# Attention and two expert layers: v's maximum in a scratch of its own, and new places for the loads and tasks of the first heads

## The chip, the core and the metric

The kernel runs on one core of a Trainium2 chip. The metric is the device time of one execution in microseconds (us). PE is the matmul engine and PEld its weight load, DVE the vector engine, ACT the scalar engine, POOL the GpSimd engine, and SP the engine whose queue issues nearly all transfers (DMAs) here. Each engine works through its own instructions in the order in which the program gives them, and waits where an input or a buffer is not ready.

## What is computed

Three parts follow one another: attention with a hashing mask, then two expert layers. Cut to what matters:

```python
q_bits = (einsum('bhsd,dk->bhsk', q, proj) > 0)      # 6 bits per row, the same for k
mask   = q_bucket[:, :, :, None] == k_bucket[:, :, None, :]
scores = where(mask, q @ k.T / sqrt(64), -1e9);  attn = softmax(scores)
x  = (attn @ v)                                       # 2 batches x 8 heads, 768 rows, 64 columns
h  = x @ w_in;   g = P(h) / (Q(h) + 1e-6);   x = g @ w_out      # 1536 x 512 x 2048
h  = x @ w2_in;  g = h - tanh(h);            out = g @ w2_out
```

## The kernel before

**Heads and places.** The attention runs over 16 heads `h` of 768 rows; each head has six blocks `j` of 128 keys. Every step of a head is a task with a number, its place: `T` holds the places of a usual head relative to its first block (six places per head), `EARLY` those of heads 0 to 3, and `MOVE` adds a correction to a single task, by name. `FILL` lists groups of idle matmuls (`fill`, L966, 122 columns each) that only keep PE busy. The tasks are sorted by place and issued in that order (`on`, L1027 and on), and each engine keeps it. So a changed number changes the order in the queues of the engines that the task touches, and nothing else.

**The steps of a head.** `load_qk` (L713) issues the load of k and q of the head (384 KB, two buffers). `split_hi` (L756, ACT) rounds them to a high part `A`, `split_lo` (L760, POOL, for head 0 DVE) makes the rest `Bl`. `place` (L768, L769) sends two parts of `A` into the operands `TBk` and `TBq`, and `out_of place` (L775, four issues) the others into `TA`. `bits` (L785, PE) makes the hash bits; `out_of bits` (L789, L792 for head 0; L795 and the transfer L798 for the others) turns them into mask rows of `TBk` and `TBq`. `smax` (L810, PE) and `out_of max` (L814, DVE) give the maximum of every row; `put_max`, for head 0 `put_half`, turns the six maxima by a PE transpose into the bank `sbank` (L825), DVE reads them out (L831), and SP sends them into a row of `TBq` (L832). Then come `scores` (L930, PE), `out_of e` (L933, ACT exponential), `round_e` (L942 ACT, L944 DVE), `rest_e` (L953, POOL) and `attend` (L985 to L988, PE). A ring of three double PSUM banks serves `bits`, `smax` and `scores`.

**v.** `load_v` (L850) loads v of two heads (384 KB), `vmax` (L854, DVE) takes each partition's maximum, `vall` (L859) sends these into one row, and `out_of vback` (L865 to L869, four small DVE instructions) makes a scale of them. It works in two numbers of `sbank`, on partition 64, in columns that lie inside the stretch which `put_part` uses on partitions 0 to 5:

```python
o = SH + D + 2 * (pr % 2)
x = sbank[64:65, o:o + 2]
```

`out_of vagain` (L873) sends the scale to all partitions; `vhi` (L894, ACT) and `vlo` (L900 or L904, ACT, then L901 on POOL or L905 on DVE) need it, and so does `vmean_of` (L911, PE), which also writes to `sbank`.

**Order on SP at the start:** `load_qk` 0, the projection, `load_v` 0, `place` 0, `load_qk` 1, `out_of place` 0, `place` 1, `vall` 0, `load_qk` 2, `out_of place` 1, the maxima of head 0 in two halves, `vagain` 0, the bits of head 1, `load_qk` 3, `place` 2, `out_of place` 2, the bits of head 2, `load_v` 1, `load_qk` 4, `place` 3.

Of the kernel before, what the change touches and what calls it, by code (L numbers as in the profile page):

```python
# [10 lines left out]
F32, F32R, F16, BF16, I32 = DT.float32, DT.float32r, DT.float16, DT.bfloat16, DT.int32  # L11
# [5 lines left out]
B, H, S, D = 2, 8, 768, 64  # L17
# [5 lines left out]
SH = S // 2  # L23
# [12 lines left out]
EH_ACT_LAST = (768, 0, 768, 384, 768, 768)  # L36
EL_DVE_LAST = (640, 0, 0, 384, 128, 768)

FILL = ((199.95, 71), (91.54, 25), (-29.26, 33), (-6.1, 72), (-0.79, 4), (-23.35, 19), (8.78, 3), (-23.45, 5), (1.45, 8))

VLO_POOL = (0, 1)

# [228 lines left out]
 'vlo 10': 0.153,  # L271
 'smax 1 3': -0.091,
 'scale 1 1': -2.1579,
 'smax 0 2': -1.278,
 'out_of e (13, 2)': -0.263,
 'load_qk 2': 3.2764,
 'vall 0': 12.2053,
 'place 1': -0.1816,
 'round_e 8 5': 0.213,
 'out_of vmean 15': 0.073,  # L280
 'out_of place 1': 0.9139,
# [5 lines left out]
 'fill 19': -1.743,  # L287
 'out_of max (0, 2)': 0.006,
 'out_of max (13, 5)': 0.393,
 'load_qk 1': 0.1764,  # L290
 'attend 8 2': -0.953,
 'load_v 0': -1.2766,
 'attend 4 2': -0.953,
# [18 lines left out]
 'normalize 15': -0.377,  # L312
 'vhi 8': -0.1387,
 'attend 12 1': -0.883,
 'vhi 2': 0.553,
 'vlo 1': 0.073,
 'out_of place 3': -0.2893,
 'scores 13 0': 0.07,
 'round_e 15 5': 0.3926,
 'vmax 0': 10.6854,  # L320
 'scores 9 1': -0.055,
 'out_of max (0, 0)': 1.02,
 'smax 0 0': 1.318,
 'out_of bits 0': 10.916,
 'out_of e (15, 1)': -0.473,
 'scores 15 1': -0.055,
 'round_e 14 4': 0.006,
 'out_of e (14, 4)': -0.01,
 'load_v 1': 2.2916,
 'put_max 15': 0.633,  # L330
 'out_of put 15': 0.625,
 'out_of max (2, 5)': -0.7062,
 'smax 2 5': -0.4082,
 'out_of e (9, 2)': -0.263,
 'attend 13 0': -0.2423,
 'halves 0 1': 0.753,
# [7 lines left out]
 'out_of e (15, 0)': 0.8687,  # L344
 'round_e 15 0': 0.3407,
 'scale 0 1': 1.277,
 'out_of max (15, 4)': -1.2373,
 'smax 15 4': -0.9393,
 'scores 15 0': 0.948,
 'put_max 1': 0.203,  # L350
 'out_of put 1': 0.155,
# [7 lines left out]
 'out_of vmean 0': 0.403,  # L359
 'vhi 12': -0.023,  # L360
 'place 0': -0.568,
 'split_hi 0': -0.27,
 'smax 1 4': -0.153,
 'out_of e (13, 5)': -0.473,
 'scores 13 5': -0.055,
 'rest_e 15 4': 2.093,
 'vmean_of 1': 0.703,
 'out_of vmean 1': 0.553,
 'bits 0': 11.964,
 'smax 0 1': 0.024,  # L370
 'join 1 1': -1.01,
 'round_e 14 5': 1.0,
 'rest_e 14 5': 0.592,
 'attend 0 3': 0.193,
 'attend 14 1': -0.008,
 'scores 15 5': 0.413,
 'scores 7 0': 0.073,
 'round_e 0 2': 0.3044,
 'scale 3 1': -0.383,
 'attend 0 4': -0.103,  # L380
 'halves 2 0': 0.203,
 'scores 1 3': -0.093,
 'halves 2 1': 0.4539,
 'round_e 15 1': -0.003}
J0 = 2
YSQ = (0.9, 4, 3.5)
GC = dict(sub=0.7, hi=1.35, lo=1.95)
# [43 lines left out]
def tile_fn(ctx: ExitStack, tc: tile.TileContext, kq, v, proj, w1i, w1o, a_, b_, w2i, w2o, out):  # L431
# [236 lines left out]
    with ExitStack() as actx:  # L668
        actx.enter_context(tc.manual_schedule(engines={getattr(nc, e).engine for e in ORDERED}))
        ap = actx.enter_context(tc.tile_pool(name="ap", bufs=1))  # L670
# [4 lines left out]
        sbank = sgl.tile([P, 512], F32, name="sbank")  # L675
# [181 lines left out]
        def vall(pr):  # L857
            row = ap.tile([1, 2 * P], F32, name=f"vrow{pr}", tag="vrow", bufs=1)
            nc.sync.dma_start(row.rearrange("o (p h) -> o p h", h=2), vmx.pop(pr))  # L859
            sc = ap.tile([1, 2], F32, name=f"vs1{pr}", tag="vs1", bufs=2)  # L860

            def back():
                o = SH + D + 2 * (pr % 2)
                x = sbank[64:65, o:o + 2]
                nc.vector.tensor_reduce(x, row.rearrange("o (p h) -> o h p", h=2), axis=AX.X, op=ALU.max)  # L865
                xi = x.bitcast(I32)
                nc.vector.tensor_scalar(xi, xi, 0x7F800000, None, op0=ALU.bitwise_and)
                nc.vector.tensor_scalar(x, x, 2.0 ** -87, 2.0 ** -12, op0=ALU.max, op1=ALU.mult)
                nc.vector.reciprocal(sc, x)  # L869

            def again():
                vs = ap.tile([P, 2], F32, name=f"vsc{pr}", tag="vsc", bufs=3)
                nc.sync.dma_start(vs, sc.unsqueeze(1).to_broadcast([1, P, 2]))  # L873
                for j in range(2):
                    vsc[2 * pr + j] = vs[:, j:j + 1]

            outs["vback", pr], outs["vagain", pr] = back, again
# [161 lines left out]
        def on(place, fn, *args):  # L1039
            tasks.append((place + MOVE.get(move_name(fn, args), 0), len(tasks), fn, args))  # L1040
# [48 lines left out]
        for u in range(NE):  # L1089
            for fi in range(FG):  # L1090
                t = end + TT["h0"] + TT["slot"] * (4 * u + fi)
                on(t, h_mm, u, fi)
                for n, f in zip("abcde", (stage_a, stage_b, stage_c, stage_d, stage_e)):
                    on(t + TT[n], f, u, fi)
        for t, n in FILL:
            on(t, fill, n)
# [27 lines left out]
        for _, _, fn, args in sorted(tasks, key=lambda x: x[:2]):  # L1124
            name = fn.__name__
# [555 lines left out]
```

## Time and profile before

| | |
|---|---|
| median of 3 runs | 750.57 us (748.86 to 751.51) |
| profiled execution | 748.52 us, span 746.8 us |
| TensorE clock, mean of the span | 0.993 of full |
| busy: PE, DVE, ACT, POOL | 729.5 us (98%), 616.5 us (83%), 551.8 us (74%), 538.4 us (72%) |
| chain that ended last | PE 74%, DVE 14%, ACT 4%, DMA 3%, POOL 2% |

A timeline row has start and length in us, engine, line, operation and tiles, and in brackets the idle time ahead of it and what ended that. A wait row names who waited for whom, with sum, count and longest. PEclk is the clock granted to PE as a share of full speed. A busy share is an average over stages with different limits, so a stage is read from its own rows.

### The profile page before, as it was taken

Reading aid. Unit: us, or ns where it says so; the run is one execution under the profiler, and the core shown is the slowest. Engines: PE = TensorE matmul, PEld = TensorE weight load, DVE = VectorE, ACT = ScalarE, POOL = GpSimd, SP = SyncE. Lnnn points to the kernel's source line nnn. Section 1 sums busy time; section 2 is a strip of 40 time slices with the busy share of each in tenths; the row PEclk is TensorE's granted clock in tenths of the full one; section 3 lists DMA queues with packets and bytes.
Section 4 is the critical chain, followed back from the end, with each engine's and each line's share of the span. In section 5 each row is a group of like instructions: output and inputs, shape, how many; then the busy total and the mean of one; then the engine's idle time right before and its main releaser. Section 6 shows DMA issues by size and latency. Waiting matters only on the chain.

```text
span 746.8 us, 14449 instructions
## 1 busy us (share of the span) xinstructions
PE 729.5 (98%) x5406; PEld 598.1 (80%) x5406; DVE 616.5 (83%) x1034; ACT 551.8 (74%) x979; POOL 538.4 (72%) x459
## 2 busy tenths in 40 slices
PE   8899999999999999999999999999999999999997
PEld 6788888888888888888888888887887676767664
DVE  7689998999968987899899999989666867778765
ACT  1688889988998787766776677688576768677652
POOL 2679898998998897777787789959646366364531
PEclk8999999999999999999999999999999999999999
DMA  7665546565420321212112212101030220311003
GB/s 197 170 163 141 151 115 173 163 150 166 124 86 30 113 85 57 70 61 69 56 57 86 75 39 70 44 2 56 29 114 32 83 85 29 113 57 57 29 29 140
DMA packets 43373, 66.56 MB, mean 89 GB/s; under 512 B 6164, under 2 KB 29812, under 8 KB 43304
## 3 DMA queue, kind: packets, MB, share of 16 engines
q1 hardware_dynamic: 43160, 65.52, 29.8%
q8 instruction: 42, 0.69, 0.4%
q14 instruction: 27, 0.22, 0.1%
q10 hardware_dynamic: 144, 0.13, 0.1%
HBM read 43.00 MB, written 3.15 MB: 62 GB/s over the span
## 4 chain that ended last, share of the span: by engine, by line
PE 74%; DVE 14%; ACT 4%; DMA 3%; POOL 2%; issue 2%; SPq 0%; POOLq 0%; ACTq 0%; DVEq 0%
PE y L1486 16%; PE h L609 16%; PE y L1179 16%; PE h2b L1391 6%; DVE mx L814 4%; PE st L930 4%; PE h2e L1391 4%; PE h2a L1391 4%; PE sm L810 2%; DVE TBk L795 1%; DVE eh L944 1%; POOL x L1365 1%; ACT e L933 1%; PE bits L785 1%; PE pv L985 1%
## 5 line engine op out<-in xcount | busy, mean ns | idle before, releaser
L953 POOL TENSOR_TENSOR el<-e,eh 128x768 f16<-128x768 f32 (+2 forms) x95 | 151.4, 1613 | 22.5 <-DVE eh L944 10.0
L1486 PE MATMUL y<-wS,g 128*128 128x512 f16 (+1 forms) x438 | 102.8, 378 | 0.0
L933 ACT ACTIVATE e<-st,lnk 128x768 f32<-128x768 f32 x96 | 86.1, 898 | 19.0 <-PE st L930 16.9
L814 DVE TENSOR_REDUCE mx<-sm 128x1 f32<-128x768 f32 x96 | 90.0, 950 | 9.5 <-PE sm L810 8.6
L1470 POOL TENSOR_TENSOR g<-tmp,g 128x384 f16<-128x384 f32 x48 | 44.0, 917 | 67.0 <-ACT g L1465 55.4
L665 POOL TENSOR_TENSOR G<-vec,G 128x512 fp32r<-128x512 f32 x44 | 57.2, 1306 | 26.0 <-ACT G L660 25.9
L1486 PEld LDWEIGHTS <-g 128*128 128x128 f16 x438 | 38.5, 98 | 45.6 <-issue 6.3
L1179 PE MATMUL y<-G,wO 128*128 128x512 f32 x288 | 67.1, 391 | 0.0
L1509 DVE SCALAR_TENSOR_TENSOR ya<-y,few,ya 128x512 f32<-128x512 f32 (+1 forms) x73 | 54.0, 741 | 15.0 <-PE y L1486 14.1
L1179 PE MATMUL y<-G,wE 128*128 128x512 f32 x288 | 66.3, 390 | 0.0
L609 PE MATMUL h<-x,wO 128*128 128x512 f32 x288 | 66.3, 390 | 0.0
L1179 PEld LDWEIGHTS y<-G,wE 128*128 128x128 f32 x288 | 54.1, 188 | 11.2
L609 PEld LDWEIGHTS h<-x,wO 128*128 128x128 f32 x288 | 54.1, 188 | 11.2
L1179 PEld LDWEIGHTS y<-G,wO 128*128 128x128 f32 x288 | 53.9, 188 | 11.3 <-POOL G L665 0.3
L942 ACT CAST eh<-e 128x384 f16<-128x384 f32 (+2 forms) x95 | 60.9, 642 | 1.7
L985 PEld LDWEIGHTS <-eh 128*128 128x128 f16 x576 | 53.1, 97 | 10.0 <-issue 9.9
L1391 PE MATMUL h2b<-x,wE 128*128 128x384 f32 x288 | 60.3, 344 | 0.8 <-ACT x L1359 0.8
L985 PE MATMUL pv<-VB,eh 128*128 128x65 f16 x540 | 57.8, 194 | 0.0
L988 PE MATMUL pv<-VB,el 128*128 128x65 f16 x540 | 57.0, 192 | 0.8 <-POOL el L953 0.8
L986 PE MATMUL pv<-VB,eh 128*128 128x64 f16 x540 | 57.4, 195 | 0.0
L930 PE MATMUL st<-TA 128*128 128x384 f32 x192 | 56.4, 375 | 0.5 <-DVE mx L814 0.3
L810 PE MATMUL sm<-TBk,TBq 76*128 76x384 f32 x192 | 52.2, 357 | 3.2 <-DVE TBq L792 2.1
(202 smaller groups left out, 2039.0 us busy)
## 6 DMA issues: line engine op xcount, KB each, us to landing
raw<-in_w1i_dram SPq DMA_DIRECT2D x16, 512.0 KB
raw<-in_w1o_dram SPq DMA_DIRECT2D x16, 512.0 KB
raw<-in_w2i_dram SPq DMA_DIRECT2D x16, 512.0 KB
raw<-in_w2o_dram SPq DMA_DIRECT2D x16, 512.0 KB
kq<-in_kq_dram SPq DMA_DIRECT2D x16, 384.0 KB
TA<-A SPq DMA_DIRECT2D x32, 192.0 KB
TA<-Bl SPq DMA_DIRECT2D x32, 192.0 KB
vraw<-in_v_dram SPq DMA_DIRECT2D x8, 384.0 KB
```

Source lines behind the costliest of these rows:

```text
L609: nc.tensor.matmul(ps, l[:, dc], r, start=(n == 0), stop=(n == 11))
L810: nc.tensor.matmul(ps[:, n], TBq[h][0:76, j * P:(j + 1) * P], TBk[h][0:76, n * SH:(n + 1) * SH], start=True, stop=True)
L814: d = nc.vector.tensor_reduce(mx[h][:, j:j + 1], ps, axis=AX.XY, op=ALU.max)
L930: nc.tensor.matmul(ps[:, n], l[h][0:k, j * P:(j + 1) * P], q[h][0:k, n * SH:(n + 1) * SH], start=(k == P), stop=(k < P))
L933: outs["e", (h, j)] = lambda: nc.scalar.activation(halved(e), ps, AF.Exp, scale=1.0 / math.sqrt(D), bias=lnk)
L942: nc.scalar.copy(t[:, 0:r], e[:, 0:r])
L953: nc.gpsimd.tensor_sub(l[:, r:NK], e[:, r:NK], eh[h, j][:, r:NK])
L985: nc.tensor.matmul(out(t), a[:, t], vb[:, j, 0:PW], start=False, stop=False, skip_group_check=True)
L986: nc.tensor.matmul(out(t)[:, 0:D], a[:, t], vb[:, j, PW:PW + D], start=False, stop=False, skip_group_check=True)
L1179: nc.tensor.matmul(ps, l[:, o], r, start=(n == 0), stop=(n == 11))
L1391: nc.tensor.matmul(banks[n, k], w_in(j, l)[:, o:o + P], x[:, r, dt], start=new and z == 0, stop=z == 5, skip_group_check=not new)
L1486: nc.tensor.matmul(ps[:, c], g[:, l, o], r[:, c], start=(z == 0), stop=(z == 5))
```

## The change

One line of code moves: the two numbers of `vback` get a small SBUF tile of their own, `vx`, in place of a corner of `sbank`. Everything else is numbers in `FILL` and `MOVE`. Sorted out by queue they do this:

- SP: `load_qk` 1 goes ahead of `place` 0, right behind `load_v` 0. `load_qk` 2 and then `vall` 0 go ahead of `place` 1. `load_v` 1 goes ahead of `out_of place` 2 and the bits of head 2. `place` 3 goes ahead of `load_qk` 4.
- PE: idle matmuls ahead of the first `bits` 71 in place of 57; 3 new ones behind the third `smax` of head 0; the groups of 4 (before the first `scores`), of 8 (behind `scores` 0 1) and of 3 go, and one single matmul comes. `scores` 0 4 goes ahead of `smax` 2 0, `scores` 0 5 ahead of `smax` 2 1 and `vmean_of` 1; `attend` 0 3 ahead of `bits` 3, `smax` 2 5 ahead of `smax` 2 4, `scores` 1 4 ahead of `vmean_of` 2. Later a few swaps in heads 6, 7 and 13 to 15: among them `smax` 15 4 ahead of `attend` 13 0, `attend` 13 4 ahead of `smax` 15 5, `put_max` 15 ahead of two `scores` and `attend` 13 5.
- ACT: `split_hi` 3 goes ahead of the exponential of block 0 1; `vhi` 2 behind the exponential of block 1 1; `vlo` 15 about two blocks earlier; one exponential of block 1 2 and one stage of the first expert layer ahead of a neighbour.
- DVE: the maximum 2 2 ahead of `vback` 1, 2 5 ahead of 2 4, the bits of head 4 ahead of a rounding, 15 4 and `vlo` 15 earlier, `out_of put` 15 earlier.
- POOL: `split_lo` 3 ahead of `rest_e` 0 1.

The diff, cut:

```diff
-FILL = ((199.95, 71), (91.54, 25), (-29.26, 33), (-6.1, 72), (-0.79, 4), (-23.35, 19), (8.78, 3), (-23.45, 5), (1.45, 8))
+FILL = ((199.95, 71), (91.54, 25), (-29.26, 52), (-6.1, 72), (-23.35, 19), (6.47, 1), (-11.01, 3))
...
- 'load_qk 2': 3.2764,
+ 'load_qk 2': -0.8365,
- 'place 1': -0.1816,
+ 'place 1': 12.6501,
- 'load_qk 1': 0.1764,
+ 'load_qk 1': -1.4262,
- 'vhi 2': 0.553,
+ 'vhi 2': 1.023,
- 'vmax 0': 10.6854,
+ 'vmax 0': 11.55,
- 'load_v 1': 2.2916,
- 'put_max 15': 0.633,
- 'out_of put 15': 0.625,
+ 'load_v 1': 2.2339,
+ 'put_max 15': -0.2439,
+ 'out_of put 15': -0.2519,
...
+ 'split_lo 0': -2.4888,
+ 'out_of max (2, 2)': -0.703,
+ 'smax 2 2': -0.405,
+ 'scores 0 4': -0.444,
+ 'vlo 15': -1.807,
+ 'out_of place 2': 4.8369,
+ 'place 3': -0.893,
+ 'split_hi 3': -1.0739,
+ 'split_lo 3': -1.0569,
+ 'scores 0 5': -0.25,
...
             def back():
-                o = SH + D + 2 * (pr % 2)
-                x = sbank[64:65, o:o + 2]
+                x = ap.tile([1, 2], F32, name=f"vx{pr}", tag="vx", bufs=2)
                 nc.vector.tensor_reduce(x, row.rearrange("o (p h) -> o h p", h=2), axis=AX.X, op=ALU.max)
```

## Rows read from the trace of the kernel before

**Rows 1.** Busy by stretch: us, then PE, PEld, DVE, ACT, POOL; PEclk, DMA, GB/s
```profile
0.00:20.00 20.00, 16.47 (x150) 14.25 (x151) 14.14 (x33) 3.78 (x4) 4.55 (x20) 0.83 0.75 196
...
60.00:80.00 20.00, 19.72 (x272) 18.27 (x269) 18.30 (x29) 18.21 (x31) 18.48 (x12) 1.00 0.64 164
```
**Rows 2.** Timeline of SP, the first 30 us: start, length, issue
```profile
0.74 0.39 SPq L713 DMA_DIRECT2D kq<-in_kq_dram  x1
...
1.65 0.43 SPq L850 DMA_DIRECT2D vraw<-in_v_dram  x1
...
5.76 0.59 SPq L713 DMA_DIRECT2D kq<-in_kq_dram  x1
...
12.14 0.46 SPq L768 DMA_DIRECT2D TBk<-A  x1
...
13.35 0.54 SPq L859 DMA_DIRECT2D vrow<-vm  x1
...
17.08 1.64 SPq L832 DMA_DIRECT2D TBq<-mr  x2
...
18.81 0.55 SPq L873 DMA_DIRECT2D vsc<-vs  x1
...
20.31 0.51 SPq L713 DMA_DIRECT2D kq<-in_kq_dram  x1
...
27.55 0.50 SPq L850 DMA_DIRECT2D vraw<-in_v_dram  x1
```
**Rows 3.** Timeline of ACT, 0 to 30 us
```profile
3.66 0.83 ACT L756 CAST A<-kq 128x768 fp32r<-128x768 f32 x1 [1.65 <-DMA kq<-in_kq_dram]
...
11.29 0.83 ACT L756 CAST A<-kq 128x768 fp32r<-128x768 f32 x1 [6.80 <-DMA kq<-in_kq_dram]
...
21.50 0.62 ACT L894 ACTIVATE VB<-vraw,vsc 128x384 f16<-128x384 f32 x1 [2.12 <-DMA vsc<-vs]
...
23.03 0.88 ACT L933 ACTIVATE e<-st,lnk 128x768 f32<-128x768 f32 x1
...
25.32 0.90 ACT L933 ACTIVATE e<-st,lnk 128x768 f32<-128x768 f32 x1 [0.87 <-PE st L930]
...
28.63 0.82 ACT L756 CAST A<-kq 128x768 fp32r<-128x768 f32 x1
```
**Rows 4.** Timeline of DVE
```profile
6.97 1.07 DVE L789 TENSOR_SCALAR TBk<-bits,thr,amp 13x768 fp32r<-13x768 f32 x1
...
16.98 0.16 DVE L869 RECIPROCAL vs<-sbank 1x2 f32<-1x2 f32 x1
...
33.60 0.95 DVE L854 TENSOR_REDUCE vm<-vraw 128x2 f32<-128x768 f32 x1 [2.10 <-DMA vraw<-in_v_dram]
...
41.96 0.96 DVE L814 TENSOR_REDUCE mx<-sm 128x1 f32<-128x768 f32 x1 [1.27 <-PE sm L810]
...
208.33 0.95 DVE L814 TENSOR_REDUCE mx<-sm 128x1 f32<-128x768 f32 x1
```
**Rows 5.** Timeline of PE
```profile
1.08 4.53 PE L966 MATMUL pvw<-ones 128*128 128x122 f16 x57 [1.08 <-DVE q1c L598]
...
8.80 1.32 PE L810 MATMUL sm<-TBk,TBq 76*128 76x384 f32 x6 [2.06 <-DVE TBq L792]
...
15.42 5.23 PE L966 MATMUL pvw<-ones 128*128 128x122 f16 x76
...
210.54 0.27 PE L825 MATMUL sbank<-ident,mx 128*6 128x128 f32 x1
```
**Rows 6.** Waits of PE in 0:60, 100:140 and 140:180: us, times, longest
```profile
PE sbank L911 <- DVE mr L831: 2.3, 1, 2.3
PE sbank L825 <- DVE vs L869: 0.5, 1, 0.5
...
PE sbank L825 <- DVE vs L869: 0.6, 1, 0.6
...
PE sbank L825 <- DVE vs L869: 0.8, 1, 0.8
```
**Rows 7.** PE's clock around its long wait, columns as in the first group
```profile
35.00:36.00 1.00, 1.00 (x14) 1.00 (x12) 1.00 (x2) 0.22 (x1) 0.00 (x0) 0.50 0.08 1
...
38.00:39.00 1.00, 1.00 (x7) 1.00 (x7) 0.77 (x3) 1.00 (x3) 0.00 (x0) 0.99 0.97 285
```

More of the change, by code (lines that the diff above doesn't have):

```diff
@@ L273 @@
  'scale 1 1': -2.1579,
- 'smax 0 2': -1.278,
+ 'smax 0 2': -1.243,
  'out_of e (13, 2)': -0.263,
- 'load_qk 2': 3.2764,
+ 'load_qk 2': -0.8365,
  'vall 0': 12.2053,
- 'place 1': -0.1816,
+ 'place 1': 12.6501,
  'round_e 8 5': 0.213,
@@ L319 @@
  'round_e 15 5': 0.3926,
- 'vmax 0': 10.6854,
+ 'vmax 0': 11.55,
  'scores 9 1': -0.055,
- 'out_of max (0, 0)': 1.02,
- 'smax 0 0': 1.318,
- 'out_of bits 0': 10.916,
+ 'out_of max (0, 0)': 1.061,
+ 'smax 0 0': 1.355,
+ 'out_of bits 0': 10.953,
  'out_of e (15, 1)': -0.473,
@@ L328 @@
  'out_of e (14, 4)': -0.01,
- 'load_v 1': 2.2916,
- 'put_max 15': 0.633,
- 'out_of put 15': 0.625,
- 'out_of max (2, 5)': -0.7062,
- 'smax 2 5': -0.4082,
+ 'load_v 1': 2.2339,
+ 'put_max 15': -0.2439,
+ 'out_of put 15': -0.2519,
+ 'out_of max (2, 5)': -1.1504,
+ 'smax 2 5': -0.8524,
  'out_of e (9, 2)': -0.263,
@@ L346 @@
  'scale 0 1': 1.277,
- 'out_of max (15, 4)': -1.2373,
- 'smax 15 4': -0.9393,
+ 'out_of max (15, 4)': -1.423,
+ 'smax 15 4': -1.125,
  'scores 15 0': 0.948,
@@ L361 @@
  'place 0': -0.568,
- 'split_hi 0': -0.27,
+ 'split_hi 0': -1.3028,
  'smax 1 4': -0.153,
@@ L368 @@
  'out_of vmean 1': 0.553,
- 'bits 0': 11.964,
- 'smax 0 1': 0.024,
+ 'bits 0': 12.001,
+ 'smax 0 1': 0.059,
  'join 1 1': -1.01,
@@ L373 @@
  'rest_e 14 5': 0.592,
- 'attend 0 3': 0.193,
+ 'attend 0 3': 0.187,
  'attend 14 1': -0.008,
@@ L378 @@
  'round_e 0 2': 0.3044,
- 'scale 3 1': -0.383,
+ 'scale 3 1': -0.377,
  'attend 0 4': -0.103,
  'halves 2 0': 0.203,
- 'scores 1 3': -0.093,
+ 'scores 1 3': -0.087,
  'halves 2 1': 0.4539,
- 'round_e 15 1': -0.003}
+ 'round_e 15 1': -0.003,
+ 'smax 8 4': 0.883,
+ 'vmean_of 2': 0.433,
+ 'split_lo 0': -2.4888,
+ 'out_of max (2, 2)': -0.703,
+ 'smax 2 2': -0.405,
+ 'round_e 1 4': 0.143,
+ 'scores 6 4': -0.433,
+ 'scores 0 4': -0.444,
+ 'put_max 2': 0.006,
+ 'out_of max (8, 4)': 0.585,
+ 'attend 6 1': -0.883,
+ 'vlo 15': -1.807,
+ 'out_of place 2': 4.8369,
+ 'round_e 1 1': 0.473,
+ 'rest_e 1 1': 0.065,
+ 'place 3': -0.893,
+ 'split_hi 3': -1.0739,
+ 'split_lo 3': -1.0569,
+ 'smax 15 5': 0.923,
+ 'out_of max (15, 5)': 0.625,
+ 'attend 7 1': -0.953,
+ 'scores 0 5': -0.25,
+ 'rest_e 14 2': 1.212,
+ 'rest_e 14 3': 0.215,
+ 'round_e 7 0': 0.008}
 J0 = 2
```

## The prediction

> **What bounds the kernel now.** I read the busy shares by stretch first. From 60 us on PE works nearly without a gap (19.72 of 20 us), with DVE, ACT and POOL close behind (18.2 to 18.5 of 20); the first 20 us have PE at 16.5 and ACT at 3.8 [rows 1]. So the start is where an engine can win time by order alone, and later an engine that gains must be followed by the others. Next I read the waits of PE. One is long: 2.3 us of `vmean_of` for DVE's read of the maxima. Three times, 0.5, 0.6 and 0.8 us, the transpose of the maxima waits for the last instruction of `vback`, which works in the same bank [rows 6]. Then I asked in the timelines why. DVE reached `vmax` of the second pair of heads 2.10 us before its data: DVE stood still until 33.60 for v, and behind it in DVE's queue stood the read of the maxima that PE waited for [rows 4]. That v had been issued at 27.55 and took 6.0 us to land [rows 2, 4]. [...] The start is a chain of loads. The second head's k and q are issued at 5.76, and ACT has them at 11.29; only then can SP issue `place` 1 at 12.14, and everything queued on SP behind it starts there: v's maximum (13.35), the maxima of head 0 (17.08), v's scale (18.81) [rows 2, 3]. ACT waits 2.12 us for that scale, until 21.50, and its first exponential is at 23.03 [rows 3].
>
> **The second head's load.** It is issued right behind v's, at 1.65 + 0.43 = 2.1 us in place of 5.76 [rows 2]. Its landing isn't in this trace. The first load is used at 3.66 [rows 3]; v and this one follow, 384 KB each, and at the 196 GB/s of the first 20 us [rows 1] each takes 2.0 us: an estimate of 7.7 us. The bounds are 5.0 (2.9 us from issue to use as the first load, 0.74 to 3.66 [rows 2, 3]) and 8.1 (6.0 us as the later v). I take 7.7: three loads then stand in one queue. ACT converts by 8.5, where it did by 12.1 [rows 3], so `place` 1 no longer holds SP. What stands between, the third head's load, v's maximum and the six transfers of `place` 1, is issued at some 0.6 us each [rows 2], all before the maxima are ready. The scale is then issued when DVE has it: 16.98 + 0.16 = 17.14 in place of 18.81, a gain of 1.67 [rows 2, 4]. It landed 2.69 us after its issue (18.81 to 21.50), and the first exponential came 1.53 later [rows 2, 3]; by this it goes from 23.03 to 21.4.
>
> Against it stand 14 more idle matmuls ahead of the first hash bits, 71 in place of 57. At 4.53/57 = 79 ns [rows 5] they are 1.1 us of PE. They end after the bits' inputs are there, and DVE reads the bits at 6.97, behind `vmax` [rows 4], so part of it is covered. I take 0.3 (0 to 1.1): the cover, DVE's work ahead, is about as long as the rest. The exponential also needs the first `scores`: PE's 76 idle matmuls run from 15.42 to 20.65, 69 ns each [rows 5]; without four of them, and 0.3 late, `scores` start at 20.7, about a microsecond ahead of 21.7. Both paths meet there. **Term A: 1.2 us** of 1.3, ends 0 and 1.6.
>
> The group of 8 idle matmuls that goes (8 x 69 ns = 0.55) stands where PE waits for buffers and DVE sets the pace, and the three new ones stand where PE waits for DVE's maxima: nothing either way, and 0.2 to 0.5 if that cover is gone.
>
> **v of the second pair.** `load_v` 1 stood behind the four transfers of `place` 2 and the bits of head 2, at 27.55. It now stands behind `place` 2's first two. The third load before these was issued at 20.31 [rows 2]; about 1.2 us earlier, and with two issues of 0.6 between, v goes out at about 21. With the 6.0 us of before it lands at 27. DVE comes to it at 33.60 - 2.10 = 31.5 [rows 4], by term A at 30.3: 3 us to spare. So DVE's wait goes. Late next is the read of the maxima itself, 0.95 us of `vmax` later; `scores` 0 5, put ahead of `vmean_of`, fills that time on PE. What PE's wait in the rows shows as 2.3 [rows 6] is thus worth DVE's 2.1. **Term B: 2.1**, ends 1.5 and 2.3.
>
> **The clock behind it.** [...] Some 3 us ran at half [rows 7], 1.5 us of PE. DVE was busy through that stretch and only then waited 1.27 us for PE, at 41.96 [rows 4]; the gain can't pass that. **Term C: 0.7**, ends 0 and 1.3.
>
> **The scratch of `vback`.** On SBUF, the transposes of the maxima need not wait for DVE's last step on it: 0.5 + 0.6 + 0.8 = 1.9 us of waits on PE [rows 6]. The four small instructions stay (the last takes 0.16 us [rows 4]). PE wins what it waited; the time at the end gains only where PE was last. DVE with 18.3 of 20 us [rows 1] has little room to follow. **Term D: 0.8**, ends 0 and 1.9.
>
> **Places further on.** Most swaps are of neighbours on PE with the same inputs: nothing, and some tenths where a buffer comes free later. `vhi` 2 goes behind an exponential on ACT, and v's second scale comes 0.96 us later on DVE, as a maximum goes ahead of it; the one covers the other. `put_max` 15 goes ahead of two `scores` and an `attend`. Its last maximum ended at 208.33 + 0.95 = 209.28, the transpose ran at 210.54 [rows 4, 5]: 1.26 us of slack, and the steps that it passes are some 2.5 us of PE. So PE may wait up to 1.3 us there, with `scores` queued behind. **Term E: -0.4**, ends 0 and -1.3.
>
> **Sum:** 1.2 + 2.1 + 0.7 + 0.8 - 0.4 = 4.4 us. From the profiled execution's 748.5 that gives 744.1. That execution lies 2.1 us under the median of the runs; I carry the difference to the median: 750.6 - 4.4 = 746.2.
>
> **Rivals.** *First, the load takes the bandwidth of what is needed sooner.* The second head's 384 KB go ahead of `place` 0, whose transfers the first `smax` needs; it ran at 8.80, released by DVE's mask rows [rows 5], so the transfers were there by then. At 196 GB/s that is 2.0 us [rows 1]; DVE's maxima, the scale and the first exponential would then all be later by up to that, and term A is gone: 4.4 - 1.2 = 3.2, 747.4 us. For it: the two stand in one queue. Against: the load issued at 5.76 took 5.5 us with 768 KB of `TA` issued behind it [rows 2, 3], more than a load alone, so what is issued later shares the engines and doesn't simply queue. [...]
>
> *Second, the other engines keep the pace.* If DVE sets the time from 40 us on, what PE alone gains (C and D) becomes idle time of PE in front of DVE's releases, and `put_max` 15 costs its whole 1.3: 1.2 + 2.1 - 1.3 = 2.0, 748.6 us. For it: DVE at 18.3 of 20 us [rows 1]. Against: DVE waited for PE too, 1.27 us at 41.96 [rows 4].
>
> *Third, slower: a load that is late takes the place of v's.* `split_hi` 3 now stands ahead of the exponential of block 0 1 on ACT, and waits for the fourth load. Before, that load was issued at 20.31 and its conversion ran at 28.63 without a wait [rows 2, 3], so it landed anywhere before that. In my schedule ACT comes to it at 22.8 and is through at 23.7, with the exponential at 24.1 in place of 25.32 [rows 3]. Every microsecond of landing after 22.8 is one more for the exponential, and with it for the buffers of `smax` and `scores` on PE. From a landing at 27.2 the whole gain is gone; at the bound of 28.6 it costs 5.8, and with PE standing still that long 1.5 more for the clock (as in C): 750.6 - 4.4 + 7.3 = 753.5 us. Against it: loads took 2.9 to 6.0 us from issue to use, and issued near 19.5 this one should land by 22.4 to 25.5.
>
> **How the numbers follow.** The forecast has 0.53, the first rival 0.17, the second 0.20, the third 0.10. About 0.3%, 2.25 us, is what a measurement of this kernel tells from no change: faster means under 748.3, slower over 752.8. The forecast counts as faster nearly throughout, the first rival mostly, the second in a third of its cases: 0.51 + 0.13 + 0.06 = 0.70. Slower is nearly the third alone: 0.09. The rest, 0.21, is no change. With all terms at their better ends the gain is 1.6 + 2.3 + 1.3 + 1.9 = 7.1, 743.5, and a microsecond for the scatter of the runs gives 742.5; that all are at their ends at once is unlikely, so no more is added. Above, the second rival with 748.6 and its scatter, and the smaller cases of the third, reach 751.0.
>
> **What would show it.** Right: SP issues the second head's load near 2 us and v's scale near 17.2; ACT's first exponential lies at 21.4 to 22; DVE's wait for v near 31 us is gone and the clock stays at full there; no transpose of the maxima waits for `vback`; DVE's maximum that was at 41.96 comes about 4 us earlier, and the first expert layer begins about 4 us earlier. Wrong: the first `smax`, at 8.80 before [rows 5], later than 9.5 us, ACT waiting for the fourth load ahead of block 0 1's exponential, or PE waiting longer for DVE or ACT between 60 and 200 us than before, with the gain at 42 us larger than that at the end.

## The result, and the profile after

The changed kernel takes 758.35 us (median of 6 runs, 755.60 to 762.55) against 749.19 us (748.51 to 751.51) for the kernel before on the same chip. The ratio is 1.012, interval 1.0098 to 1.0143: slower by some 9 us, where 746.2 with 742.5 to 751.0 was forecast. The profiled execution, the slowest of the six (762.55 us), has a span of 760.7 us, against 746.8; so its rows show somewhat more loss than the median has.

First the page after: busy time by engine, and the chain of work that ended last, by engine. The lines have moved by 24 or 25 places (L825 is L850 now, L609 is L633 or L634).

```profile
PE 736.6 (97%) x5409; PEld 601.3 (79%) x5409; DVE 630.6 (83%) x1034; ACT 551.8 (73%) x979; POOL 539.1 (71%) x459
...
PE 66%; DVE 20%; ACT 5%; POOL 4%; issue 2%; DMA 2%; ACTq 0%; DVEq 0%; POOLq 0%
```

DVE executes the same 1034 instructions as before and is busy 630.6 us in place of 616.5. These 14.1 us are new, and DVE's share of the chain has gone from 14% to 20%. Which instructions grew? Groups of DVE instructions by line and shape, the mask and the scaling before and then all four after: name, shape and count, then busy us in all and mean ns of one.

```profile
L867 DVE TENSOR_SCALAR sbank<-sbank 1x2 int32<-1x2 int32 x8 | 1.4, 172 | 0.3
L868 DVE TENSOR_SCALAR sbank<-sbank 1x2 f32<-1x2 f32 x8 | 1.4, 172 | 0.3
...
L892 DVE TENSOR_SCALAR vx<-vx 1x2 f32<-1x2 f32 x8 | 11.9, 1484 | 0.3
L891 DVE TENSOR_SCALAR vx<-vx 1x2 int32<-1x2 int32 x8 | 5.4, 671 | 0.3
L889 DVE TENSOR_REDUCE vx<-vrow 1x2 f32<-1x256 f32 x8 | 3.2, 401 | 0.1
L893 DVE RECIPROCAL vs<-vx 1x2 f32<-1x2 f32 x8 | 1.2, 153 | 0.3
```

The last four are the small instructions of `vback`. The reduction and the reciprocal take what they took (0.16 us for the reciprocal in [rows 4]). The mask (L891) and the scaling (L892), two numbers each, were 172 ns each in every one of their eight places before; now they are 671 and 1484 ns on average, 17.3 us in place of 2.8. These 14.5 us cover the whole growth of DVE. The timeline says what they wait for. Two stretches of DVE and POOL, after: start and length in us.

```profile
17.95 0.41 DVE L889 TENSOR_REDUCE vx<-vrow 1x2 f32<-1x256 f32 x1
17.97 1.80 POOL L785 TENSOR_TENSOR Bl<-kq,A 128x768 fp32r<-128x768 f32 x1 [6.03 <-ACT A L781]
18.39 1.40 DVE L891 TENSOR_SCALAR vx<-vx 1x2 int32<-1x2 int32 x1
19.83 0.16 DVE L892 TENSOR_SCALAR vx<-vx 1x2 f32<-1x2 f32 x1
...
38.59 0.16 DVE L891 TENSOR_SCALAR vx<-vx 1x2 int32<-1x2 int32 x1
38.73 1.65 POOL L977 TENSOR_TENSOR el<-e,eh 128x768 f16<-128x768 f32 x1 [1.10 <-ACT eh L966]
38.78 1.61 DVE L892 TENSOR_SCALAR vx<-vx 1x2 f32<-1x2 f32 x1
```

At 18.39 the mask begins while POOL is inside an instruction that ends at 19.77; the mask ends at 19.79. Then POOL stands still, and the scaling takes 0.16. At 38.59 it is the other way round: POOL is idle during the mask (0.16), starts at 38.73, and the scaling that begins 0.05 us later ends with POOL, at 40.39. The reduction at 17.95 isn't held, though POOL works through most of it. So on SBUF these two instructions stand still for as long as POOL's current instruction runs. Ten of the sixteen are hit, for 1.40 to 1.76 us each, and each of the ten ends within 0.03 us of a POOL instruction's end. The other six take 0.16: two fall into idle time of POOL, four into the tenth of a microsecond in which one POOL instruction gives way to the next.

PE's waits show who pays. Stretch 60 to 260 us, one row before and two after: us in all, times, longest.

```profile
PE sbank L911 <- DVE mr L831: 0.7, 1, 0.7
...
PE sbank L935 <- DVE mr L856: 5.0, 4, 2.4
PE sbank L850 <- DVE mx L839: 2.6, 1, 2.6
```

The old waits of the transpose for `vback` [rows 6] are gone, as intended. In their place PE waits longer for what is queued behind `vback` on DVE: the maxima and their read-out. One such chain, DVE and PE, after:

```profile
58.13 1.76 DVE L891 TENSOR_SCALAR vx<-vx 1x2 int32<-1x2 int32 x1
59.92 1.56 DVE L892 TENSOR_SCALAR vx<-vx 1x2 f32<-1x2 f32 x1
...
62.45 0.27 DVE L856 TENSOR_SCALAR mr<-sbank 6x128 fp32r<-6x128 f32 x1
62.77 0.54 PE L935 MATMUL sbank<-VB,ones 128*128 128x64 f16 x12 [2.38 <-DVE mr L856]
```

Both `tensor_scalar` are held, the read-out stands behind them, and PE waits 2.38 us for it. In this execution the clock falls behind such waits: it is 0.50 from 64 to 66 us, and again from 197 us, behind the wait of 2.6 us. PE by stretches, after, columns as in [rows 1]:

```profile
40.00:60.00 20.00, 18.83 (x203) 15.83 (x203) 18.40 (x28) 15.26 (x25) 15.26 (x11) 0.91 0.46 125
60.00:80.00 20.00, 17.62 (x216) 16.51 (x212) 17.31 (x29) 14.66 (x24) 15.65 (x10) 0.91 0.47 123
...
180.00:200.00 20.00, 17.06 (x230) 15.35 (x227) 18.90 (x30) 14.05 (x23) 15.70 (x11) 0.92 0.45 121
```

From 60 to 80 us PE is busy 17.62 us at a mean clock of 0.91, where it was 19.72 at 1.00 [rows 1]. The clock is not the whole loss: the fastest of the six executions after takes 755.60 us at a mean clock of 0.995, no lower than the 0.993 of the kernel before.

### The profile page after: what moved, and what is told of

It reads as the page before. It is cut to its first block, busy times and chain, and to the rows that moved or that the text cites. A ratio compares the mean times of both kernels' runs of the same rounds, so it can differ in the third digit from the quotient of the medians.

```text
span 760.7 us, 14451 instructions
## 1 busy us (share of the span) xinstructions
PE 736.6 (97%) x5409; PEld 601.3 (79%) x5409; DVE 630.6 (83%) x1034; ACT 551.8 (73%) x979; POOL 539.1 (71%) x459
## 4 chain that ended last, share of the span: by engine, by line
PE 66%; DVE 20%; ACT 5%; POOL 4%; issue 2%; DMA 2%; ACTq 0%; DVEq 0%; POOLq 0%
PE y L1510 16%; PE h L634 12%; PE y L1203 11%; PE h2b L1415 6%; DVE mx L839 5%; PE st L954 4%; PE h2e L1415 4%; PE h2a L1415 4%; PE sm L835 2%; PE bits L810 2%; DVE vx L892 2%; PE pvw L990 1%; DVE eh L968 1%; POOL G L690 1%; DVE TBk L820 1%
## 5 line engine op out<-in xcount | busy, mean ns | idle before, releaser
L977 POOL TENSOR_TENSOR el<-e,eh 128x768 f16<-128x768 f32 (+2 forms) x95 | 152.0, 1617 | 31.9 <-DVE eh L968 17.3
L1533 DVE SCALAR_TENSOR_TENSOR ya<-y,few,ya 128x512 f32<-128x512 f32 (+1 forms) x73 | 54.0, 741 | 14.9 <-PE y L1510 14.1
L634 PE MATMUL h<-x,wO 128*128 128x512 f32 x288 | 66.3, 389 | 0.0
L634 PEld LDWEIGHTS h<-x,wO 128*128 128x128 f32 x288 | 54.1, 188 | 11.2
L835 PE MATMUL sm<-TBk,TBq 76*128 76x384 f32 x192 | 54.0, 367 | 6.5 <-DVE TBq L817 2.6
```

The costliest lines, as they stand in the source:

```text
L634: nc.tensor.matmul(ps, l[:, dc], r, start=(n == 0), stop=(n == 11))
L835: nc.tensor.matmul(ps[:, n], TBq[h][0:76, j * P:(j + 1) * P], TBk[h][0:76, n * SH:(n + 1) * SH], start=True, stop=True)
L977: nc.gpsimd.tensor_sub(l[:, r:NK], e[:, r:NK], eh[h, j][:, r:NK])
```

## Experiments

### The scratch or the places

`scratch_only` is the kernel before with the new tile and nothing else; `places_only` is the changed kernel with the scratch back in its corner of `sbank`.

```diff
 scratch_only, from the kernel before
-                o = SH + D + 2 * (pr % 2)
-                x = sbank[64:65, o:o + 2]
+                x = ap.tile([1, 2], F32, name=f"vx{pr}", tag="vx", bufs=2)
 places_only, from the kernel after
-                x = ap.tile([1, 2], F32, name=f"vx{pr}", tag="vx", bufs=2)
+                o = SH + D + 2 * (pr % 2)
+                x = sbank[64:65, o:o + 2]
```

> The kernel before with nothing but the scratch of vback on SBUF. Theory P: 756 to 762 us, with most of the tensor_scalar pairs showing one or two stretches of 1.4 to 1.8 us that end where a POOL instruction ends. Theory Q: 747 to 750 us, as the three waits of the transpose for vback (1.9 us) go.

> All new places and fills, with the two numbers of vback back in the corner of sbank. Theory P (the scratch): on SBUF the two tensor_scalar of vback stand still while a POOL instruction runs (1.4 to 1.8 us in place of 0.16), 14 us of DVE in sum; without it the places alone give 744 to 750 us, both instructions take 0.17 us and DVE's busy time falls from 630.6 to about 616.5 us. Theory Q (the places): the longer first fill, the second head's load ahead of place 0 and the third head's conversion ahead of an exponential cost the time; then it stays at 755 us or more.

The scratch alone gives 763.04 us, ratio 1.0176 (1.0138 to 1.0215), the places alone 747.22, ratio 0.9965 (0.9948 to 0.9982). The first lies a microsecond above the 756 to 762 expected, the second within its range. So the one line of code costs 11 us on the new places (758.35 less 747.22) and 13 on the old (763.04 less 749.73), and the numbers win 2.5. In `places_only`, with the scratch in PSUM, POOL doesn't hold the two instructions. Its timeline, DVE and POOL:

```profile
54.16 1.83 POOL L785 TENSOR_TENSOR Bl<-kq,A 128x768 fp32r<-128x768 f32 x1
54.25 0.17 DVE L892 TENSOR_SCALAR sbank<-sbank 1x2 int32<-1x2 int32 x1
54.46 0.17 DVE L893 TENSOR_SCALAR sbank<-sbank 1x2 f32<-1x2 f32 x1
```

The same operations run in 0.17 us each in the middle of POOL's instruction. What differs is where the two numbers lie.

### Which form is held

`single` keeps the scratch on SBUF and all new places, but works one number at a time.

```diff
-                nc.vector.tensor_scalar(xi, xi, 0x7F800000, None, op0=ALU.bitwise_and)
-                nc.vector.tensor_scalar(x, x, 2.0 ** -87, 2.0 ** -12, op0=ALU.max, op1=ALU.mult)
+                for k in range(2):
+                    nc.vector.tensor_scalar(xi[:, k:k + 1], xi[:, k:k + 1], 0x7F800000, None, op0=ALU.bitwise_and)
+                    nc.vector.tensor_scalar(x[:, k:k + 1], x[:, k:k + 1], 2.0 ** -87, 2.0 ** -12, op0=ALU.max, op1=ALU.mult)
```

> The changed kernel with its scratch on SBUF, but each tensor_scalar of vback done on one number at a time (four instructions in place of two, the same result). [...] If any tensor_scalar from SBUF to SBUF has to wait for a running POOL instruction, the first of the four is stretched as before and a second may be, and the time stays at 756 to 764 us.

It takes 745.07 us, ratio 0.9944 (0.9923 to 0.9965), and not the 756 to 764 expected for a wait of any `tensor_scalar`. Its DVE groups by shape:

```profile
L893 DVE TENSOR_SCALAR vx<-vx 1x1 f32<-1x1 f32 x16 | 2.3, 142 | 0.5
L892 DVE TENSOR_SCALAR vx<-vx 1x1 int32<-1x1 int32 x16 | 2.2, 137 | 0.3
```

Twice as many instructions, 4.5 us in place of 17.3. In its timeline, POOL and DVE, four of them run inside a POOL instruction of 36.94 to 38.58:

```profile
36.94 1.64 POOL L978 TENSOR_TENSOR el<-e,eh 128x768 f16<-128x768 f32 x1 [0.69 <-ACT eh L967]
...
37.26 0.14 DVE L892 TENSOR_SCALAR vx<-vx 1x1 int32<-1x1 int32 x1
37.44 0.14 DVE L893 TENSOR_SCALAR vx<-vx 1x1 f32<-1x1 f32 x1
37.51 0.13 DVE L892 TENSOR_SCALAR vx<-vx 1x1 int32<-1x1 int32 x1
37.67 0.14 DVE L893 TENSOR_SCALAR vx<-vx 1x1 f32<-1x1 f32 x1
```

So it isn't SBUF as such, and not `tensor_scalar` as such: it is the `tensor_scalar` that reads two numbers from SBUF and writes two there. Nor is every one-input operation on SBUF held. In the changed kernel the reciprocal of the same two numbers takes 0.15 us at 88.81, inside a POOL instruction of 88.72 to 90.37, and the casts `eh<-e` of 128x384 take 0.53 to 0.56 us inside POOL's instructions and outside. What sets these apart was not tested.

By the mean, the scaling of two numbers on SBUF takes 1484 ns in the changed kernel, of one number 142 in `single`, and of two numbers in PSUM 172 in the kernel before; the reduction takes 401. By what way POOL's instruction holds the one form back, no run here shows.

### Another corner of the same bank

If the transpose waited for `vback` because both write the same columns, other columns would do. `low_only` is the kernel before and `places_low` the one after, with the scratch in columns 0 to 3, which `put_part` doesn't use.

```diff
-                o = SH + D + 2 * (pr % 2)
+                o = 2 * (pr % 2)
```

> The kernel before with the two numbers in columns 0 to 3 of sbank, nothing else. Theory P: small instructions of 0.17 us, no wait of a transpose for vback; the 1.9 us of PE are worth 0 to 1.9 us at the end, 747 to 750 us. Theory Q says the same of this run.

> All new places, the two numbers in other columns of sbank (0 to 3, which only vlo uses): off the columns of the maxima, yet in PSUM. Theory P: neither the stretch on DVE nor the wait of the transpose, 742 to 749 us, up to 1.9 us under the run with the corner of before. Theory Q: 754 us or more.

The wait stays. PE's waits in `low_only`:

```profile
PE sbank L825 <- DVE vs L869: 1.7, 3, 0.6
```

1.7 us in three waits, against 0.5 + 0.6 + 0.8 in [rows 6]; 750.25 us, ratio 1.0003 (0.9984 to 1.0022). `places_low` keeps two such waits (1.0 us) and gives 747.88, ratio 0.9971 (0.9956 to 0.9987), no better than `places_only`. Against what I expected, other columns of the same tile don't remove the wait; a tile of its own does (no such wait in `single`). A tile of its own in PSUM wasn't tried.

### The first loads, one at a time

`v1_only` is the kernel before with one move in SP's queue (two entries of `MOVE`): the second pair's v loads ahead of `place` 2's last transfers. `fills57` is `places_only` with 57 first idle matmuls in place of 71, and `kq1_back` is `fills57` with the second head's load behind `place` 0 again.

```diff
 v1_only, from the kernel before
- 'load_v 1': 2.2916,
+ 'load_v 1': 2.2339,
+ 'out_of place 2': 4.8369,
 fills57, from places_only: in FILL
-(-29.26, 52)
+(-29.26, 38)
 kq1_back, from fills57
- 'load_qk 1': -1.4262,
+ 'load_qk 1': 0.1764,
```

> The kernel before with one move: v's second load ahead of out_of place 2. Term B and C of the prediction taken alone: DVE's wait of 2.1 us for v goes and the clock stays up near 35 us; 2.1 to 2.8 us less than before, 746.5 to 748 us. If what is won there is lost again further on, 749 to 750 us.

> The new places with the scratch in its old corner (747.2 us), and 57 idle matmuls ahead of the first hash bits as before, in place of 71. If they are what made the start late, the bits run near 5.5 us, the first smax near 8.8 to 9.3 and the first exponential 1 to 1.5 us earlier than 23.0: 745.5 to 746.5 us. If the transfers of place 0, behind the second head's load, are what is late, the first smax stays at 10.3 to 11.2, waits for a DMA, and the time stays at 747 to 748 us.

> As the run with 57 idle matmuls, and the second head's load behind place 0 again; the third head's load and v's maximum stay ahead of place 1. If the load took the bandwidth of place 0, the first smax goes back to 8.8 us and waits for DVE's mask rows, v's scale goes out near 17.2, and the time is 745 to 746.5 us. If it did not, this is 747 to 749 us, as ACT gets the second head at 11 to 12 us again.

`v1_only` takes 747.59 us, ratio 0.9969 (0.9955 to 0.9983). DVE's timeline there:

```profile
32.10 0.94 DVE L855 TENSOR_REDUCE vm<-vraw 128x2 f32<-128x768 f32 x1
...
39.98 0.96 DVE L815 TENSOR_REDUCE mx<-sm 128x1 f32<-128x768 f32 x1 [0.61 <-PE sm L811]
```

v's maximum no longer waits (2.10 us in [rows 4]), the clock has a mean of 1.00 from 20 to 40 us (0.91 in the kernel before, 0.50 at 35 in [rows 7]), and the maximum that stood at 41.96 comes at 39.98. This one load gives 2.2 of the 2.5 us that all the places give.

`fills57` gives 748.38 (ratio 0.9984, 0.9971 to 0.9997) and `kq1_back` 748.15 (0.9983, 0.9971 to 0.9995): with or without the second head's load first, the same time. PE's first `smax` in `fills57`, and then in `kq1_back`:

```profile
10.48 1.73 PE L835 MATMUL sm<-TBk,TBq 76*128 76x384 f32 x6 [3.57 <-DMA TBq<-A]
```

```profile
9.07 1.32 PE L835 MATMUL sm<-TBk,TBq 76*128 76x384 f32 x6 [2.06 <-DVE TBq L817]
```

With the load first, the transfers of `place` 0 land late and `smax` waits 3.57 us for them; with it behind, `smax` runs 1.4 us earlier, but ACT gets the second head at 11.67 in place of 8.97 and v's row comes late: DVE waits 1.31 us for it at 17.52. The first exponential lies at 22.60 and 23.26. Each order trades one wait for the other. So `fills57` came out by its second expectation, 0.4 us above it in time, and `kq1_back` mixes both: the `smax` of the first, the time of the second.

### The scratch that isn't held, on the old places

Does term D stand by itself? `single_only` is the kernel before with the one-number scratch, `v1_single` the same with v's early load.

```diff
 single_only, from the kernel before
-                o = SH + D + 2 * (pr % 2)
-                x = sbank[64:65, o:o + 2]
+                x = ap.tile([1, 2], F32, name=f"vx{pr}", tag="vx", bufs=2)
 and the loop over one number at a time as in single
 v1_single: single_only and v1_only together
```

> The kernel before with the scratch of vback on SBUF, and its two tensor_scalar done on one number at a time (four instructions, every place as before). It leaves out nothing. [...] Rival (the scratch outside the bank lengthens the kernel by itself, whatever form the operations have): slower, as with two numbers at a time, by several us and above 752.

> The kernel before with two edits: the load of the second pair's v ahead of place 2's last transfers, and the scratch on SBUF worked one number at a time. It leaves out nothing. If the gains of the two add: 2.2 (v's load alone) plus what single_only shows (0 to 1.9) less than before, 745.5 to 747.5, with neither DVE's wait for v near 31 us nor a wait of a transpose for vback. Rival (the remaining new places of the changed kernel carry part of the gain of 4.7 us that they and this scratch had together): 747 to 748, no better than v's load alone.

Term D's 0 to 1.9 us give 747.9 to 749.8 for `single_only`, and 745.5 to 747.5 was the forecast for `v1_single`. Both were missed: 753.61 us, ratio 1.0050 (1.0031 to 1.0069), and 750.69, ratio 1.0012 (1.0000 to 1.0024). Yet no instruction of `vback` is held in them (137 to 142 ns each), and PE waits for no `vback`. The rival's number for `single_only` came (above 752), but not its reason. PE's timeline where the first expert layer takes over, the kernel before and then `single_only`:

```profile
243.73 11.13 PE L609 MATMUL h<-x,wE 128*128 128x512 f32 x48
...
238.48 3.95 PE L966 MATMUL pvw<-ones 128*128 128x122 f16 x71
245.72 13.85 PE L609 MATMUL h<-x,wE 128*128 128x512 f32 x48 [3.29 <-DVE g L655]
```

Up to here it is ahead: the 71 idle matmuls end at 242.43, in the kernel before at 243.73. But then `h` waits 3.29 us for a DVE step of the expert layer, which it did not before. PE's clock behind this wait, `single_only`, columns as in [rows 1]:

```profile
242.00:244.00 2.00, 0.43 (x9) 0.26 (x5) 1.97 (x4) 0.42 (x1) 0.00 (x0) 1.00 0.03 5
...
246.00:248.00 2.00, 2.00 (x5) 1.53 (x5) 1.55 (x3) 1.29 (x3) 2.00 (x3) 0.50 0.21 39
248.00:250.00 2.00, 2.00 (x6) 1.60 (x5) 0.69 (x1) 0.21 (x1) 2.00 (x3) 0.50 0.77 246
```

The 48 matmuls take 13.85 us, 11.13 before. A gain of 1.3 us was turned into a loss of 4.3 in the profiled execution, behind a wait in a stage that the edit doesn't touch. `h` takes a PSUM bank of a ring of seven, and in these programs that bank had last held a tile that DVE still had to read. Eight kernels at this point, from their traces; "ready" is the start of `h` less its wait:

| kernel | first idle matmuls | ready | wait | start of `h` | span |
|---|---|---|---|---|---|
| before | 57 in 4.53 us | 243.73 | none | 243.73 | 746.8 |
| v1_only | 57 in 4.48 | 240.91 | none | 240.91 | 744.0 |
| single_only | 57 in 5.38 | 242.43 | 3.29 | 245.72 | 751.1 |
| v1_single | 57 in 5.86 | 240.43 | 3.26 | 243.69 | 746.5 |
| scratch_only | 57 in 5.04 | 252.95 | 1.15 | 254.10 | 758.1 |
| places_only | 71 in 6.26 | 239.98 | 1.13 | 241.11 | 745.0 |
| single | 71 in 6.28 | 239.00 | 1.12 | 240.12 | 744.1 |
| after | 71 in 6.06 | 256.82 | none | 256.82 | 760.7 |

The built programs say which tile that was. `h` has the same bank in all thirteen kernels; what differs is the tile that last held it in the attention's ring of three double banks. Where that is `xT`, the last transpose of the attention, which was read earlier (before, after, `v1_only`, `low_only`, `single_swap`), there is no wait. Where it is `low`, a scratch of the weight decoding (`scratch_only`, `places_only`, `places_low`, `fills57`, `kq1_back`, `single`), `h` waits 1.12 to 1.15 us for the DVE step that reads it and writes `wt`. Where it is `hr`, a scratch of the expert layer (`single_only`, `v1_single`), it waits 3.26 to 3.29 us for the DVE step that reads it and writes `g`.

In `v1_single` the wait is as long, but the clock held in the profiled execution (1.00 from 242 to 250 us, `h` 11.18 us); its median lies 4.2 us above its span, 3 in the kernel before. The mean clock of the other eleven executions is 0.991 to 0.995, of this one 0.995; where in their spans it fell isn't seen.

To test that the bank and not the work makes this wait, `single_swap` takes `single` and does both masks first, then both scalings. PE's queue is the same, instruction by instruction; in the program, though, the first `h` now waits for DVE and PE, where in `single` it waits for DVE alone. The expectation has another bank for this; it is the same bank with another last tile, `xT` in place of `low`.

```diff
 single_swap, from single
                 for k in range(2):
                     nc.vector.tensor_scalar(xi[:, k:k + 1], xi[:, k:k + 1], 0x7F800000, None, op0=ALU.bitwise_and)
+                for k in range(2):
                     nc.vector.tensor_scalar(x[:, k:k + 1], x[:, k:k + 1], 2.0 ** -87, 2.0 ** -12, op0=ALU.max, op1=ALU.mult)
```

> The changed kernel with the SBUF scratch worked one number at a time, as in `single`, but with the two masks first and the two scalings behind them; it leaves out nothing, and every other instruction stands in its queue as in `single`. In the program the first matmul of the first expert layer behind the 71 idle ones (`h`, L634) now waits for other engines than in `single`, so it has another of the ring's seven PSUM banks. Theory (what the bank held before decides whether PE waits there, and the order of two tiny instructions decides the bank through the allocation alone): the wait of h for DVE's wt, 1.1 us in `single`, is gone, as in the kernel before; the head end lies where it did (h ready at 239.0 to 239.2 us, so that it starts there in place of 240.1), and the span is about 1 us shorter, 743. Rival (DVE's weight decoding sets the pace there, and PE waits for it later anyway): the wait of h is gone, but its us comes back as a later wait of h or y for wt, and the span stays at 744.

It takes 743.64 us (741.17 to 744.40), ratio 0.9914 (0.9897 to 0.9930): the lowest median of all, though its interval overlaps that of `single` (0.9923 to 0.9965). PE's timeline at the same place, `single` and then `single_swap`:

```profile
240.12 11.22 PE L634 MATMUL h<-x,wE 128*128 128x512 f32 x48 [1.12 <-DVE wt L535]
```

```profile
236.90 11.13 PE L634 MATMUL h<-x,wE 128*128 128x512 f32 x48
```

The wait is gone and doesn't come back as a wait for DVE's weights later. Nor does `h` need what the step for `wt` makes: here it starts at 236.90, and that step ends at 238.08. The profiled spans differ by 4.4 us, the medians by 1.4. Of the 4.4, 1.12 is this wait; 1.0 lies in the first 71 idle matmuls (5.28 us against 6.28), ahead of the edit. I count as shown that the wait is gone, and not what that is worth in the median; why the rest of this execution is shorter stays open.

## Why the prediction was wrong

**The step that failed** is in term D: "The four small instructions stay (the last takes 0.16 us [rows 4])". I priced the moved instructions by a row from PSUM, and by the reciprocal alone, as if the place of an operand didn't enter their time. It does: 2.8 us became 17.3. That cost is on DVE, which I had called the engine with "little room to follow" in the same paragraph; the end of the attention moved from a ready time of 239.00 (`single`) to 256.82, by 17.8 us in the profiled executions (13.3 in the medians, 758.35 less 745.07). DVE's added time, 17.3 less the 4.5 us of the one-number form, is 12.8. How much of it reached the end, and how much came from PE's waits and the clock at 0.91 and 0.92, isn't sorted out. Term D's range, 0 to 1.9, left out the side below nothing without a reason.

**Term D without that**, the transposes' waits gone, was about right in size, at the ready time: earlier by 0.98 us (`places_only` to `single`), 1.30 (before to `single_only`) and 0.48 (`v1_only` to `v1_single`), with 0.8 forecast. The first idle matmuls differ by up to 1.4 us between these executions, so the three agree no closer than that. At the end of the kernel it came, if anywhere, in `single` (745.07 against 747.22 for `places_only`); in the other two the wait of `h` ate it up.

**Terms B and C**, v's load and the clock behind it, were right together: 2.1 + 0.7 = 2.8 forecast, 2.82 measured at the ready time of `v1_only`, and 2.2 in the medians. What C took for granted, that PE's clock stays up without the wait, is seen in `v1_only`: 1.00 from 20 to 40 us, 0.91 in the kernel before.

**Term A**, the second head's load, is the term that gave least, though its first links are there. In `places_only` SP issues the load at 2.12, ACT converts from 8.29 on, 0.83 us (through by 8.5 was forecast), and `place` 1 no longer holds SP. Over the six kernels with this order ACT has the load at 7.74 to 9.32, where I took 7.7 with 8.1 as the bound. But v's scale is issued at 18.56 and not at 17.14, and the first exponential starts at 23.02 and not at 21.4. In five kernels with the new places and a scratch that isn't held (`places_only`, `places_low`, `fills57`, `single`, `single_swap`) it starts at 21.61 to 23.34, in five with the old order of loads (before, `low_only`, `v1_only`, `v1_single`, `single_only`) at 23.03 to 23.98. The second one starts at 24.53 to 26.40 against 25.32 to 26.26, and there hardly anything is left. Two steps failed. The 14 more idle matmuls took PE to 7.16 at the first `bits` of `places_only`, 5.42 before: 1.7 us in that execution, where I took 0.3 and held 1.1 for the bound, as 71 took 88 ns each there and not 79. And with fewer of them the first rival's case comes in their place: `place` 0 lands late, 3.57 us of wait in `fills57`, and 3.67 in `places_low`, where the 71 took only 5.26 us. The rival had 0.17; that `place` 0 lands late behind the load holds there, though no run shows whether by the bandwidth, and the row that I set against it came from an order in which no second head's load stood ahead of these transfers.

**Term E** cost nothing that shows: in `single` no transpose waits for a maximum, and the places beyond v's load bring 0.93 us more at the ready time (240.91 to 239.98), with 1.13 given back in the wait of `h`.

**The second rival**, other engines keep the pace, didn't come by its own terms: PE's gains of `v1_only` reach the end (2.82 at `h`, 2.8 in the span). In the changed kernel DVE does set more of the pace, 20% of the chain that ended last in place of 14%, but by the held instructions. **The third**, the slower one, wasn't the mechanism: in the changed kernel `split_hi` 3 waits 0.80 us at 26.36, by the profile for a transfer out of `A` and not for the load, and the exponential behind it starts at 27.10, but `places_only` with the same order is faster than before. So slower came about by a way that I hadn't listed. Two of the signs that I had named for being wrong are there in the changed kernel, the first `smax` at 10.81 and PE's longer waits for DVE between 60 and 200 us; but the first is there in `places_only` too (10.32), which is faster than before. Without the held form the same sum would have been near: 745.07 for `single`, with 746.2 forecast. That is in part luck: term A gave hardly anything, term E cost nothing, and the wait of `h`, which I hadn't thought of, took 1.1 us back.

## What to carry to other kernels

When an operand moves between PSUM and SBUF, price the instruction anew for the new place: look at what each of its operands is, and at what POOL does at that moment, not at its old duration. Here a two-number `tensor_scalar` on SBUF stood until POOL's instruction ended, 1.40 to 1.76 us in ten cases of sixteen; one number at a time (137 and 142 ns on average), or PSUM (172 ns), avoided it. And after an edit look at the next stage's first wait for a buffer, even where nothing was changed: its bank may now come from a tile that is read later, which here made waits of 1.1 to 3.3 us, as much as the edit won or more.

## What was not expected of the hardware

- The held instructions that began at 18.39 and 38.78 ended within 0.02 us of POOL's, and moved only two numbers: so small an operand was no protection.
- The same 57 idle matmuls at the start took 4.48 to 5.86 us in different executions, and 71 took 5.26 to 6.28. Landmarks of two traces can't be compared closer than that unless these took the same time in both.
